# Fetching the first queries and keys in transfers of their own, on two queues, with other planning figures

## The chip, the cores and the metric

The program runs on one core of one Trainium2 chip. The metric is the device time of one execution in microseconds; less is better. In the profile PE is the tensor engine (PEld its weight loads), DVE VectorE, ACT ScalarE, POOL GpSimd, and SP the engine that issues transfers.

## What is computed

Attention with two sparse masks, then two networks on its output, all in float32:

```python
# q, k, v: (4, 8, 576, 64)
scores = scale * q @ k.T                      # per batch and head
mask_local   = (rel >= 0) & (rel < 32)        # heads 0 to 3, rel = query - key
mask_strided = (rel >= 0) & (key % 32 == query % 32)   # heads 4 to 7
attn = softmax(where(mask, scores, -1e9)) @ v
x = attn as (2304, 512)
h = maximum(maximum(x @ w1, x @ w2), x @ w3)  # 512 -> 768
x = h @ w_out                                 # 768 -> 512
h = x @ w_in                                  # 512 -> 2048
g = maximum(h, 0) + alpha * minimum(h, 0)
out = g @ w_out2                              # 2048 -> 512
```

## The kernel before

**Stages.** The program has three stages that share the engines in time. In the first, the attention of the four batches is woven with the first network ("gates": `w1`, `w2`, `w3` with their maximum; "mix": `w_out`) of batches 0 to 2 and with the conversion of the weights. Then the first network of batch 3 runs alone (`first_net`). In the last stage, from 403 us on, the second network runs in three blocks of 768 rows, whose products are written as seven per block and quarter (`h_products`) and followed by the output products (`o_units`). Products that have to be exact are done as three products of a high and a low part, so most matrices are split: a cast on ACT makes the high part, a subtraction on DVE the low one (L237 and L240 in the first stage).

**Attention.** It runs in units `(b, cc, hf)`: batch, a pair of heads, and half of the queries. Pairs 2 and 3 are the strided ones, 0 and 1 the local ones; the order of units in a batch is `ATT_UNITS` (2,0), (2,1), (3,0), (3,1), (0,0), (1,0), (0,1), (1,1). The strided queries and keys are stored by residue, so that a group of 6 or 7 residues is a block of 108 or 126 columns: three groups of 108 (324 columns) make the first half, two of 126 (252 columns) the second. A unit goes through scores on PE (L304), mask and row minimum on DVE (L312), exponential on ACT (L319), reciprocal on DVE (L330), scaling of `e` by `rc` on DVE or ACT (L252, L250), transposes on PE (L345), a copy `pt` to memory on either engine (L237), products with the values on PE (L370), and the split into `x` (L237, L240).

**Weights.** They arrive as 64-bit floats: a transfer `raw` (L413, three buffers), a word conversion on ACT (L427), a join on DVE (L431, L433), then the split into `w` (L237, L240). A gate group is twelve products of 288 columns (L530) with one weight tile; after it ACT or DVE takes the result into `t` (L616, L619). A group of the mix is 18 products (L552).

**What sets the order.** In the first stage a planner, `Weave`, sets it. Every piece of work is a task with an engine and a cost, a position `pos`, the events that it needs and gives, and the buffers that it makes and uses. `run` goes through time: among the tasks that are ready it takes, on the engine that is free first, the one with the smallest position, and emits its instructions there and then. `DELAY` is the time that the plan adds between the end of a task and its use elsewhere. Each engine then works through its own list in order. Buffers turn over in rings, eight banks of PSUM among them. All transfers are issued by SP, in the order of the plan, and wait there in line. The first is `alpha`, the slopes of the second network, which DVE negates into `nalpha` at the start of the last stage.

Of the kernel before, what the change touches and what calls it, by code (L numbers as in the profile page):

```python
# [2 lines left out]

# [19 lines left out]
NA = S // STRIDE  # L23
# [15 lines left out]
NUNITS = 2 * (3 * NF1 + NCC)  # L39
# [4 lines left out]
class Weave:  # L44
# [6 lines left out]

    DELAY = {"PE": 300, "ACT": 250, "DVE": 250, "SP": 2300}

    URGENT = 1000

    def __init__(self, rings):
# [33 lines left out]
                    at = max(at, done[u])  # L92
        return at

    def run(self):
        free = dict.fromkeys(self.DELAY, 0)
        left = [sum(len(self.givers[e]) for e in task[3]) for task in self.tasks]
        takers = {}
        for t, task in enumerate(self.tasks):
            for e in task[3]:  # L100
                for g in self.givers[e]:
                    takers.setdefault(g, []).append(t)
        at = [0] * len(self.tasks)
        ready = {t for t, n in enumerate(left) if not n}
        done, mode = {}, None
        while ready:
            options = {}
            for t in ready:
                engines, _, pos, _, makes, m, slack = self.tasks[t]
                when = self.place(makes, done)  # L110
                if when is None:
                    continue
                when = max(when, at[t] + slack)
                best = None
                for e, cost in engines:
                    start = max(when, free[e])
                    if best is None or start + cost < best[0] + best[2]:
                        best = (start, e, cost)
                start, e, cost = best
                if m is not None:  # L120
                    start += 100 * (m != mode)
                options.setdefault(e, []).append((start, pos - (m is not None and m == mode), t, cost))
            pick = None
            for e, c in options.items():
                first = min(o[0] for o in c)
                o = min((o for o in c if o[0] <= first + 120), key=lambda o: (o[1], o[0], o[2]))
                if pick is None or o[0] < pick[1][0]:
                    pick = (e, o)
            e, (start, _, t, cost) = pick
            _, emit, _, _, makes, m, _ = self.tasks[t]  # L130
            ready.remove(t)
            emit(e)
            for ring, key in makes:
                self.made[ring].append(key)
            mode = mode if m is None else m
            free[e] = start + cost
            done[t] = start + cost + self.DELAY[e]
            for u in takers.get(t, ()):
                left[u] -= 1
                same = e == "PE" == self.tasks[u][0][0][0]  # L140
                at[u] = max(at[u], start + cost if same else done[t])
                if not left[u]:
                    ready.add(u)
        assert len(done) == len(self.tasks)


@with_exitstack
def attention_maxout_prelu_kernel(
# [13 lines left out]
    nc = tc.nc  # L162
# [106 lines left out]
    def load_task(b, cc, pos):  # L269
        qk, vk = ("q", b, cc), ("v", b, cc)  # L270

        def emit_qk(_):
            q = qkp.tile([P, S], F32, tag="q", name="q")
            nc.sync.dma_start(q, qT[b, cc])
            k = qkp.tile([P, S + 32 * (cc < 2)], F32, tag="k", name="k")
            nc.sync.dma_start(k, kTl[b, cc] if cc < 2 else kTs[b, cc - 2])
            tl[qk] = q, k

        def emit_v(_):
            v = tl[vk] = vp.tile([P, 6 if cc < 2 else 5, 2, D], F32, tag="v", name="v")  # L280
            nc.sync.dma_start(v, vl[b, cc] if cc < 2 else vs[b, cc - 2])

        add(load(592), emit_qk, pos, gives=[qk], makes=[("q", qk)])
        add(load(350), emit_v, pos + 1, gives=[vk], makes=[("v", vk)])

    def attention_tasks(b, cc, hf, pos, step):
# [76 lines left out]
        def values(_):  # L363
# [6 lines left out]
                    nc.tensor.matmul(pv[D * j:D * (j + 1), nq * i:nq * (i + 1)], v[:nk, t, j, :],  # L370
                                     tl["pt", u, j][:nk, nq * i:nq * (i + 1)], start=True, stop=True)

        add((("PE", 2 * n * 85),), values, pos + 2 * step, needs=[vk] + [("pt", u, j) for j in range(2)],
            gives=[pvk], makes=[("bank", pvk)] + [("x", k) for k in fresh],
            uses=[vk] + [("pt", u, j) for j in range(2)] + xks, mode="values", slack=slack)

        def parts(h):
# [336 lines left out]

    homes = [("gate", f, g) for f in range(NF1) for g in range(3)] + [("mix", f) for f in range(NF1)]
    build_constants()
    nc.sync.dma_start(alpha_sb, alpha)
    for b in range(B):
        first, last = (-40, -8) if b == 0 else ((b - 1) * NUNITS + (16 if b == 1 else 3), b * NUNITS - 3)
        step = (last - first) / (len(ATT_UNITS) + 2)  # L720
        for i, (cc, hf) in enumerate(ATT_UNITS):
            if i in (0, 2, 4, 5):
                load_task(b, cc, first + step * i - 8)
            attention_tasks(b, cc, hf, first + step * i, step)
# [45 lines left out]
    ps_h = ctx.enter_context(tc.tile_pool(name="ps_h", bufs=2, space=PSUM, reuse_waits="tile"))  # L770
    ps_o = ctx.enter_context(tc.tile_pool(name="ps_o", bufs=6, space=PSUM, reuse_waits="tile"))
    NH = DM // 2
    nalpha = osp.tile([P, NF2], F32, name="nalpha")
    nc.vector.tensor_scalar(out=nalpha, in0=alpha_sb, scalar1=-1.0, scalar2=None, op0=ALU.mult)
    gts, kept, accs, res = {}, {}, {}, {}
# [300 lines left out]
```

## Time and profile before

| | |
|---|---|
| three timed runs | 770.6, 774.55, 776.38 us, median 774.55 |
| profiled execution | 772.29 us, its span 770.2 us |
| busy in the span | PE 97%, DVE 77%, ACT 59% |
| first matmul | 5.25 us |
| start of the last stage | 403.24 us |

Times inside the execution count from the start of the span. The profiled execution's own time is 2.1 us more than its span. Busy shares are means over stages with different limits; windows show the stages apart.

### The profile page before, as it was taken

The numbers are of one execution on the slowest core, as the hardware profiler recorded it, in microseconds if no ns is written. First come the engines' busy times: TensorE is split into PE (matmuls) and PEld (weight loads), VectorE is DVE, ScalarE is ACT, GpSimd is POOL, SyncE is SP. The second block draws the span as 40 slices with busy tenths as digits, with TensorE's granted clock in tenths as the row PEclk, the third lists the DMA queues.
The fourth block names the chain that finished last, engine by engine and source line by source line (L and its number), as shares of the span: only waits on it lengthen the run. The fifth ranks groups of instructions, "written<-read, shape, count | busy, mean of one in ns | idle before, by whom it ended". The sixth has DMA issues, their size and how long they took to land.

```text
span 770.2 us, 16100 instructions
## 1 busy us (share of the span) xinstructions
PE 744.1 (97%) x5704; PEld 723.2 (94%) x5704; DVE 594.6 (77%) x1658; ACT 457.9 (59%) x1238; POOL 3.2 (0%) x16
## 2 busy tenths in 40 slices
PE   5899999999989999999999999999999999999997
PEld 4689898999989999999999999999999999999997
DVE  5899998779777796326457988878888877888884
ACT  6997796656768487304246566634656644556561
POOL 1000000000000000000000000000000000000000
PEclk9899999999999999999999999999999999999999
DMA  7467768876879865365947789999888999877361
GB/s 243 157 233 250 222 233 289 297 247 247 291 262 310 274 205 170 120 243 209 342 157 249 264 290 304 381 393 364 286 286 311 347 403 327 271 250 255 119 204 53
DMA packets 85471, 199.37 MB, mean 259 GB/s; under 512 B 10640, under 2 KB 40848, under 8 KB 85392
## 3 DMA queue, kind: packets, MB, share of 16 engines
q1 hardware_dynamic: 85392, 198.35, 74.7%
q8 instruction: 45, 0.74, 0.4%
q14 instruction: 34, 0.28, 0.1%
HBM read 148.51 MB, written 49.81 MB: 258 GB/s over the span
## 4 chain that ended last, share of the span: by engine, by line
PE 60%; DVE 17%; DMA 10%; ACT 8%; issue 3%; SPq 1%; DVEq 0%; ACTq 0%
PE ph L947 20%; PE po L790 15%; PE bank L530 14%; PE bank L552 7%; DMA wh<-w 4%; ACT e L319 2%; DVE word L433 2%; DVE g L784 2%; DMA raw<-in_w 2%; DVE c L794 2%; DVE w L240 2%; PE bank L304 1%; DVE word L431 1%; DVE t L619 1%; PE bank L370 1%
## 5 line engine op out<-in xcount | busy, mean ns | idle before, releaser
L530 PE MATMUL bank<-x,w 128*128 128x288 f32 x1728 | 236.8, 297 | 4.5 <-DVE x L240 1.4
L530 PEld LDWEIGHTS bank<-x,w 128*128 128x128 f32 x1728 | 231.3, 189 | 6.7 <-ACT pt L237 1.7
L947 PE MATMUL ph<-x,w 128*128 128x384 f32 x1008 | 203.3, 337 | 1.1 <-DVE c L952 1.1
L790 PE MATMUL po<-w,g 128*128 128x256 f32 x1296 | 183.8, 282 | 1.7 <-DVE g L784 0.6
L790 PEld LDWEIGHTS po<-w,g 128*128 128x128 f32 x1296 | 175.5, 189 | 4.2 <-DVE g L784 3.2
L947 PEld LDWEIGHTS ph<-x,w 128*128 128x128 f32 x1008 | 168.3, 188 | 2.1 <-DVE c L952 1.8
L952 DVE TENSOR_TENSOR c<-ph,c 128x384 f32<-128x384 f32 x168 | 90.8, 553 | 33.1 <-PE ph L947 32.2
L783 ACT CAST g<-c 128x384 fp32r<-128x384 f32 x96 | 48.5, 505 | 89.7 <-DVE c L934 56.5
L552 PE MATMUL bank<-h,w 128*128 128x288 f32 x576 | 79.5, 297 | 0.4 <-DVE t L619 0.4
L552 PEld LDWEIGHTS bank<-h,w 128*128 128x128 f32 x576 | 76.8, 188 | 1.5 <-DVE t L619 0.6
L240 DVE TENSOR_TENSOR w<-word,w 128x512 fp32r<-128x512 f32 x88 | 55.4, 635 | 26.8 <-ACT w L237 26.5
L319 ACT ACTIVATE e<-e,nm 96x128 f32<-96x128 f32 (+2 forms) x176 | 67.9, 392 | 8.1 <-DVE nm L312 8.0
L904 ACT ACTIVATE c<-c 128x384 f32<-128x384 f32 x96 | 50.4, 525 | 34.0 <-DVE c L952 33.0
L237 ACT CAST w<-word 128x512 fp32r<-128x512 f32 x88 | 50.8, 582 | 31.8 <-DMA wh<-w 15.9
L905 ACT ACTIVATE c<-c,nalpha 128x384 f32<-128x384 f32 x96 | 59.2, 617 | 3.1
L908 DVE SCALAR_TENSOR_TENSOR c<-c 128x384 f32<-128x384 f32 x96 | 52.9, 551 | 8.9 <-ACT c L905 8.9
L784 DVE TENSOR_TENSOR g<-c,g 128x384 fp32r<-128x384 f32 x96 | 52.7, 549 | 1.9 <-ACT g L783 1.9
L784 DVE TENSOR_TENSOR g<-k,g 128x384 fp32r<-128x384 f32 x72 | 36.7, 548 | 14.4 <-ACT g L783 14.4
L427 ACT ACTIVATE word<-raw 128x512 f32<-128x512 f32 x56 | 37.2, 676 | 9.6 <-DMA raw<-in_w 4.8
L433 DVE SCALAR_TENSOR_TENSOR word<-raw,word 128x512 uint32<-128x512 uint32 x56 | 38.8, 692 | 1.9
L619 DVE TENSOR_TENSOR t<-bank,t 128x288 f32<-128x288 f32 x72 | 32.3, 449 | 7.6 <-PE bank L530 4.1
L783 ACT CAST g<-k 128x384 fp32r<-128x384 f32 x72 | 33.4, 516 | 7.8 <-PE po L790 4.4
(72 smaller groups left out, 683.3 us busy)
## 6 DMA issues: line engine op xcount, KB each, us to landing
w<-wh SPq DMA_DIRECT2D x72, 512.0 KB, 4.9
raw<-in_w SPq DMA_DIRECT2D x50, 512.0 KB, 4.6
w<-wo SPq DMA_DIRECT2D x48, 512.0 KB, 5.8
w<-wp SPq DMA_DIRECT2D x36, 512.0 KB, 6.0
wh<-w SPq DMA_DIRECT2D x24, 512.0 KB, 3.5
xd<-xst SPq DMA_DIRECT2D x28, 384.0 KB, 3.3
x<-xd SPq DMA_DIRECT2D x28, 384.0 KB, 8.1
wp<-w SPq DMA_DIRECT2D x24, 256.0 KB, 3.2
```

Of the source, the lines that this page charges most:

```text
L240: nc.vector.tensor_tensor(out=out_, in0=x, in1=y, op=ALU.subtract)
L319: nc.scalar.activation(tl[ek][:nq, j, i, :nk], tl[ek][:nq, j, i, :nk], AF.Exp, bias=tl["nm", u][:nq, j, i:i + 1], scale=-1.0, accum_out=tl ...
L433: nc.vector.scalar_tensor_tensor(out=a, in0=raw[:, :, 0], scalar=29, in1=a, op0=ALU.logical_shift_right, op1=ALU.bitwise_or)
L530: nc.tensor.matmul(acc, words["gate", f, g][:, wi, cc * P:(cc + 1) * P], xt[b, cc, hf][:, xi, :], start=n == 0, stop=n == 3 * NCC - 1)
L552: nc.tensor.matmul(acc, words["mix", f][:, wi, dc * P:(dc + 1) * P], st["h", hf, f][:, xi, :], start=n == 0, stop=n == 3 * NF1 - 1)
L783: nc.scalar.copy(g[:, 0], x)
L784: return g, lambda: nc.vector.tensor_tensor(out=g[:, 1], in0=x, in1=g[:, 0].bitcast(F32), op=ALU.subtract)
L790: nc.tensor.matmul(bank[:, NH * half:NH * (half + 1)], g[:, gi, t * P:(t + 1) * P], w[:, wi, off:off + NH], start=first and i == 0, stop=l ...
L905: nc.scalar.activation(a, a, AF.Copy, scale=nalpha[:, f:f + 1])
L908: nc.vector.scalar_tensor_tensor(out=a, in0=h, scalar=0.0, in1=a, op0=ALU.max, op1=ALU.add)
L947: nc.tensor.matmul(bank, words["h", n, i][:, wi, off + c * P:off + (c + 1) * P], x2h[blk, k, c][:, xi, :], start=m == 0, stop=m == 5)
L952: nc.vector.tensor_tensor(out=out_, in0=bank, in1=other, op=ALU.add)
```

## The change

Four things. The two transfers for the queries and keys of the first unit's pair, (0, 2), are cut at column 324: the first 324 columns of the queries are SP's first transfer and those of the keys ACT's first instruction; the other 252 columns follow on SP. `alpha` is fetched at the start of the last stage instead of the start of the program. The planner's hand-over time from ACT and DVE is 350 instead of 250, and the positions of batch 0's attention begin at -32 instead of -40. And the value products of a strided pair's second half now need those of its first half. `plan` also takes arguments for other settings; here they keep their defaults, and the random sway is zero.

```diff
-    DELAY = {"PE": 300, "ACT": 250, "DVE": 250, "SP": 2300}
...
+    def plan(self, seed=None, near=120, change=100, slack=1.0, delay=350, shift=0.0):
+
+        rng = random.Random(seed)
+        sway = [rng.uniform(-shift, shift) if task[2] > -self.URGENT / 2 else 0.0 for task in self.tasks]
+        delays = {"PE": 300, "ACT": delay, "DVE": delay, "SP": 2300}
...
-            nc.sync.dma_start(q, qT[b, cc])
             k = qkp.tile([P, S + 32 * (cc < 2)], F32, tag="k", name="k")
-            nc.sync.dma_start(k, kTl[b, cc] if cc < 2 else kTs[b, cc - 2])
+            source = kTl[b, cc] if cc < 2 else kTs[b, cc - 2]
+
+            cut = RG[3][0] * NA if (b, cc) == (0, 2) else 0
+            if cut:
+                nc.sync.dma_start(q[:, :cut], qT[b, cc][:, :cut])
+                nc.scalar.dma_start(k[:, :cut], source[:, :cut])
+            nc.sync.dma_start(q[:, cut:], qT[b, cc][:, cut:])
+            nc.sync.dma_start(k[:, cut:], source[:, cut:])
...
-        add((("PE", 2 * n * 85),), values, pos + 2 * step, needs=[vk] + [("pt", u, j) for j in range(2)],
-            gives=[pvk], makes=[("bank", pvk)] + [("x", k) for k in fresh],
+        begun = ("x begun", b, cc)
+        add((("PE", 2 * n * 85),), values, pos + 2 * step,
+            needs=[vk] + [("pt", u, j) for j in range(2)] + ([begun] if cc >= 2 and hf else []),
+            gives=[pvk] + ([begun] if cc >= 2 and not hf else []), makes=[("bank", pvk)] + [("x", k) for k in fresh],
...
-    nc.sync.dma_start(alpha_sb, alpha)
     for b in range(B):
-        first, last = (-40, -8) if b == 0 else ((b - 1) * NUNITS + (16 if b == 1 else 3), b * NUNITS - 3)
+        first, last = (-32, -8) if b == 0 else ((b - 1) * NUNITS + (16 if b == 1 else 3), b * NUNITS - 3)
...
     NH = DM // 2
+    nc.sync.dma_start(alpha_sb, alpha)
     nalpha = osp.tile([P, NF2], F32, name="nalpha")
```

What this does to the lists of the engines shows at three places. Line numbers after the change are higher: L320 are scores, L361 transposes, L386 value products, L548 gates, L570 the mix.

SP's list at the start of the program, before and then after; `in_qT` and `in_kTs` are the queries and the strided keys, `in_vs` the values.

```order
L717 DMA alpha_sb<-in_alpha 128x16
L274 DMA q<-in_qT 128x576
L276 DMA k<-in_kTs 128x576
L281 DMA v<-in_vs 128x640
L274 DMA q<-in_qT 128x576
L276 DMA k<-in_kTs 128x576
```

```order
L289 DMA q<-in_qT 128x324
L291 DMA q<-in_qT 128x252
L292 DMA k<-in_kTs 128x252
L297 DMA v<-in_vs 128x640
L291 DMA q<-in_qT 128x576
L292 DMA k<-in_kTs 128x576
```

The transfer of alpha is gone from the first place, the first queries are there in its stead, and the first 324 columns of keys are missing from the list, since ACT issues them; all that follows keeps its place.

PE's list at the end of batch 0's attention, before and then after: transposes (`ident,e`), value products (`pt,v`), scores (`k,q`) and the gates (`x,w`).

```order
L530 MATMUL bank<-x,w 128x288 x12
L370 MATMUL bank<-pt,v 64x96 x6
L304 MATMUL bank<-k,q 126x126 x4
L530 MATMUL bank<-x,w 128x288 x12
L345 MATMUL bank<-ident,e 128x96 x6
L304 MATMUL bank<-k,q 108x108 x6
L370 MATMUL bank<-pt,v 64x96 x6
L530 MATMUL bank<-x,w 128x288 x156
```

```order
L548 MATMUL bank<-x,w 128x288 x12
L386 MATMUL bank<-pt,v 64x96 x6
L361 MATMUL bank<-ident,e 128x96 x6
L320 MATMUL bank<-k,q 126x126 x4
L320 MATMUL bank<-k,q 108x108 x6
L386 MATMUL bank<-pt,v 64x96 x6
L548 MATMUL bank<-x,w 128x288 x228
```

One gate group less stands ahead of the last value products, and the run of gates behind them is 228 products long instead of 156.

PE's list at the end of batch 2's attention (the second boundary between batches), before and then after; `h,w` is the mix.

```order
L304 MATMUL bank<-k,q 108x108 x6
L370 MATMUL bank<-pt,v 64x96 x12
L345 MATMUL bank<-ident,e 128x96 x12
L530 MATMUL bank<-x,w 128x288 x12
L370 MATMUL bank<-pt,v 64x96 x12
L552 MATMUL bank<-h,w 128x288 x54
L530 MATMUL bank<-x,w 128x288 x24
```

```order
L320 MATMUL bank<-k,q 108x108 x6
L386 MATMUL bank<-pt,v 64x96 x12
L361 MATMUL bank<-ident,e 128x96 x12
L570 MATMUL bank<-h,w 128x288 x18
L386 MATMUL bank<-pt,v 64x96 x12
L570 MATMUL bank<-h,w 128x288 x54
L548 MATMUL bank<-x,w 128x288 x96
```

Between the transposes and the last value products there is now a group of the mix instead of a gate group. At the first boundary, a batch earlier, the new list has four score products between the transposes and the gate group, where there was nothing.

## Rows read from the trace of the kernel before

**Rows 1.** Windows: start:end, length, busy PE, PEld, DVE, ACT, POOL, PEclk, DMA, GB/s.

```profile
5.25:44.48 39.23, 31.73 (x278) 24.93 (x278) 31.84 (x196) 34.95 (x150) 0.00 (x0) 0.91 0.61 206
44.48:125.20 80.72, 78.36 (x654) 74.58 (x655) 76.47 (x231) 65.91 (x198) 0.00 (x0) 1.00 0.74 246
```

**Rows 2.** Waits of PE, 30 to 420 us: total, times, longest.

```profile
PE bank L345 <- DVE t L619: 1.4, 1, 1.4
PE bank L530 <- DVE x L240: 1.4, 1, 1.4
PE bank L530 <- ACT pt L237: 1.3, 2, 1.1
PE bank L345 <- ACT e L250: 1.0, 2, 0.6
```

**Rows 3.** Timeline, first 8 us: start, duration, engine, operation, idle time before it.

```profile
0.74 0.40 SPq L717 DMA_DIRECT2D alpha_sb<-in_alpha  x1
1.20 0.42 SPq L274 DMA_DIRECT2D q<-in_qT  x1
1.67 0.42 SPq L276 DMA_DIRECT2D k<-in_kTs  x1
...
3.08 0.43 SPq L276 DMA_DIRECT2D k<-in_kTs  x1
...
3.91 0.33 POOL L188 TENSOR_SCALAR_AFFINE_SELECT mask_s<-mask_s 128x126 f32<-128x126 f32 x1
...
5.25 2.30 PE L304 MATMUL bank<-k,q 64*108 64x108 f32 x20 [5.25 <-DMA k<-in_kTs]
...
7.11 0.38 ACT L319 ACTIVATE e<-e,nm 108x108 f32<-108x108 f32 x1 [5.09 <-DVE nm L312]
```

**Rows 4.** Issues up to 2 us, then to 3.5: size, us from issue to landing.

```profile
q<-in_qT SPq DMA_DIRECT2D x1, 288.0 KB, 3.1
k<-in_kTs SPq DMA_DIRECT2D x1, 288.0 KB, 3.5
alpha_sb<-in_alpha SPq DMA_DIRECT2D x1, 8.0 KB, 1.7
...
k<-in_kTs SPq DMA_DIRECT2D x1, 288.0 KB, 5.0
```

**Rows 5.** Groups by shape on ACT, 7.1 to 41.8 us: busy, mean ns, idle before.

```profile
L319 ACT ACTIVATE e<-e,nm 108x108 f32<-108x108 f32 x17 | 6.3, 373 | 5.1 <-DVE nm L312 5.1
...
L427 ACT ACTIVATE word<-raw 128x512 f32<-128x512 f32 x5 | 3.3, 670 | 0.0
...
L250 ACT ACTIVATE e<-e,rc 96x128 f32<-96x128 f32 x9 | 3.0, 397 | 0.0
...
L237 ACT COPY pt<-bank 128x288 f32<-128x288 f32 x4 | 1.5, 387 | 0.3 <-PE bank L345 0.2
...
L250 ACT ACTIVATE e<-e,rc 126x126 f32<-126x126 f32 x2 | 0.7, 400 | 0.0
```

**Rows 6.** Timeline of ACT and PE at the end of batch 0's attention.

```profile
41.45 0.38 ACT L237 COPY pt<-bank 128x288 f32<-128x288 f32 x1
...
44.48 20.68 PE L530 MATMUL bank<-x,w 128*128 128x288 f32 x154 [0.81 <-DVE w L240]
```

**Rows 7.** Timeline of PE: a score group, then the second and third boundary.

```profile
65.65 0.71 PE L304 MATMUL bank<-k,q 64*126 64x126 f32 x8
...
222.05 3.13 PE L530 MATMUL bank<-x,w 128*128 128x288 f32 x12 [1.08 <-ACT pt L237]
...
314.84 2.66 PE L552 MATMUL bank<-h,w 128*128 128x288 f32 x18
```

**Rows 8.** Timeline of SP, PE and DVE at the start of the last stage.

```profile
388.77 15.45 SPq L563 DMA_DIRECT2D x<-xo  x12
...
403.24 6.44 PE L947 MATMUL ph<-x,w 128*128 128x384 f32 x36
...
405.59 0.56 DVE L952 TENSOR_TENSOR c<-ph,c 128x384 f32<-128x384 f32 x1 [4.22 <-PE ph L947]
```

More of the change, by code (lines that the diff above doesn't have):

```diff
@@ L1 @@
 import math
+import random
 from contextlib import ExitStack
@@ L93, in place @@
         return at
-    def run(self):
-        free = dict.fromkeys(self.DELAY, 0)
-        left = [sum(len(self.givers[e]) for e in task[3]) for task in self.tasks]
[L98 to L102, printed above, removed]
+    def plan(self, seed=None, near=120, change=100, slack=1.0, delay=350, shift=0.0):
+        rng = random.Random(seed)
+        sway = [rng.uniform(-shift, shift) if task[2] > -self.URGENT / 2 else 0.0 for task in self.tasks]
+        delays = {"PE": 300, "ACT": delay, "DVE": delay, "SP": 2300}
+        self.made = {ring: [] for ring in self.rings}
+        free = dict.fromkeys(delays, 0)
+        left = [sum(len(self.givers[e]) for e in task[3]) for task in self.tasks]
         at = [0] * len(self.tasks)
         ready = {t for t, n in enumerate(left) if not n}
-        done, mode = {}, None
+        done, mode, order = {}, None, []
         while ready:
@@ L108, in run @@
             for t in ready:
-                engines, _, pos, _, makes, m, slack = self.tasks[t]
+                engines, _, pos, _, makes, m, wait = self.tasks[t]
                 when = self.place(makes, done)
@@ L112, in run @@
                     continue
-                when = max(when, at[t] + slack)
+                when = max(when, at[t] + slack * wait)
                 best = None
@@ L120, in run @@
                 if m is not None:
-                    start += 100 * (m != mode)
-                options.setdefault(e, []).append((start, pos - (m is not None and m == mode), t, cost))
+                    start += change * (m != mode)
+                options.setdefault(e, []).append(
+                    (start, pos + sway[t] - (m is not None and m == mode), t, cost))
             pick = None
@@ L125, in run @@
                 first = min(o[0] for o in c)
-                o = min((o for o in c if o[0] <= first + 120), key=lambda o: (o[1], o[0], o[2]))
+                o = min((o for o in c if o[0] <= first + near), key=lambda o: (o[1], o[0], o[2]))
                 if pick is None or o[0] < pick[1][0]:
@@ L129, in run @@
             e, (start, _, t, cost) = pick
-            _, emit, _, _, makes, m, _ = self.tasks[t]
+            makes, m = self.tasks[t][4:6]
             ready.remove(t)
-            emit(e)
+            order.append((t, e))
             for ring, key in makes:
@@ L136, in run @@
             free[e] = start + cost
-            done[t] = start + cost + self.DELAY[e]
-            for u in takers.get(t, ()):
+            done[t] = start + cost + delays[e]
+            for u in self.takers.get(t, ()):
                 left[u] -= 1
@@ L144, in run @@
         assert len(done) == len(self.tasks)
+        return order
+    def run(self, **settings):
+        self.takers = {}
+        for t, task in enumerate(self.tasks):
+            for e in task[3]:
+                for g in self.givers[e]:
+                    self.takers.setdefault(g, []).append(t)
+        for t, e in self.plan(**settings):
+            self.tasks[t][1](e)
 @with_exitstack
```

## The prediction

> **What bounds the kernel now.** I read the windows first [rows 1]. Between 44.48 and 125.20 the tensor engine (PE) is busy 78.36 of 80.72 us. The stage ahead of that is different: of the 39.23 us from the first matmul at 5.25 to 44.48 PE shows 31.73 us, at a mean granted clock of 0.91, while ScalarE (ACT) shows 34.95 and VectorE (DVE) 31.84. So the head of the program is a chain of scores, masks, exponentials and copies that ACT carries, and PE becomes the bound at 44.48. From there one run of 154 gate products takes 20.68 us, 134 ns each [rows 6]. The list of waits [rows 2] then says what PE loses from 30 to 420: single waits of up to 1.4 us. A gain can come from two places only, the head and those waits. The order of the last stage does not change, apart from one new wait, for alpha.
>
> The profiled execution took 772.29 us with a span of 770.2; the median of the three timed runs is 774.55, 2.3 us above it. I sum differences on the profiled execution and apply them to the median. The three runs spread from 770.6 to 776.38, so about 1% (7.7 us) is what a measurement can tell from no change.
>
> **Part 1, the first transfers.** Now SyncE (SP) issues alpha at 0.74, q at 1.20 and k at 1.67 [rows 3]; they land after 1.7, 3.1 and 3.5 us [rows 4], so k is there at 5.17 and PE starts at 5.25. After the change the first 324 of 576 columns of q are SP's first issue (0.74), and the same part of k is ACT's first instruction, at about the same moment, ahead of its table load. A 288 KB transfer lands after 3.1 us and an 8 KB one after 1.7, so 280 KB cost 1.4 us, 5 ns per KB. Both parts are 162 KB: 1.7 + 324 x 0.005 = 3.3 us, landing at 0.74 + 3.3 = 4.0. That is an estimate from these two rows. First matmul at 4.1 instead of 5.25: 1.15 us earlier. The ends: 2.0 us (each part for itself, 0.74 + 2.5 = 3.2) and 0 (no row shows a transfer from ACT's queue; it may be as late as k is now). I take the case that counts all bytes. The mask is finished at 3.91 + 0.33 = 4.24 [rows 3], and DVE starts on it well over a microsecond after PE, so it does not replace the wait. The second group of scores needs the other 252 columns, SP's second and third issues: by then the same 576 KB have been moved, by about 5.2, when PE is just through with the first group.
>
> Not all of this survives. The third group of scores needs the next q and k, whose places in SP's queue do not move (the k's is at 3.08); that k lands 5.0 us after its issue [rows 4], at 8.1. From a first score matmul to its first exponential it takes 7.11 - 5.25 = 1.86 us [rows 3], so ACT gets the third group at 8.1 + 1.86 = 9.95. Now it comes to it after ten exponentials of 0.373 us [rows 5], at 7.11 + 3.73 = 10.84. So 0.9 us of the earlier start are kept, however early the first transfers land.
>
> The rows also say that k lands 0.87 us after q (5.17 against 4.30), though it is issued only 0.47 later [rows 3 and 4]. The Trainium skill, "DMA: Bandwidth & Descriptors", section "Issuing engines are not separate DMA queues", says that the transfers of all issuing engines run on the same 16 DMA engines, and that a second issuing engine saves only the time of the issue. By that rule the use of ACT's queue alone would be worth one issue slot, 0.47 us, and the trace agrees as far as one queue can show it: the lag between q and k is data and not issue. By the rule alone the sum below would be some 0.4 us smaller.
>
> **Part 2, the new order in the head.** The planner now assumes 350 instead of 250 for a hand-over from ACT or DVE and places batch 0 later, so the order changes everywhere up to the last batch. In the head I compare what ACT does up to its last copy of batch 0's probabilities, which ends at 41.45 + 0.38 = 41.83 now [rows 6]. Counted in the two orders, the new one has 14 instead of 16 exponentials of 108x108, 4 instead of 5 word conversions, 6 instead of 4 copies of 128x288, and scalings of e by rc of 0 instead of 2 (126x126) and 6 instead of 9 (96x128); all other kinds are equal in number. With the means of [rows 5]: -2 x 0.373 - 0.67 + 2 x 0.387 - 2 x 0.400 - 3 x 0.397 = -2.6 us. Durations overlap a little with the next instruction's, so I take four fifths, 2.1 us (ends: 2.6, and 0 if ACT waits more than now). The last copy then ends at 41.83 - 0.9 - 2.1 = 38.8; the value products follow, some 0.7 us (an estimate, as long as the score group of [rows 7]), and the unbroken run of gates, 228 long in the new order, starts at 39.5. By then 12 gate products are done; the old order had 26 at 44.48. The 26th would be at 39.5 + 14 x 0.134 = 41.4, so the head gains 44.48 - 41.4 = 3.1 us, of which 0.9 is part 1. The five scalings have moved to DVE, which has two copies fewer for them and 7.4 us idle in that stretch [rows 1]; that hides them. Without that cover they are up to 2.0 us (0.40 each on ACT).
>
> What is late next is the supply of weights: each needs a join and a subtraction on DVE, and DVE shows 76.47 of 80.72 us in the stretch after 44.48 [rows 1]. The old run used its first three weights twice before it needed the fourth; so does the new one (five groups of twelve, 8.0 us). So the margin stays about what it is, if DVE's list is as far ahead as ACT's. That is the weakest step.
>
> **Part 3, the batch boundaries.** At the first one PE waits 1.4 us for x [rows 2]. The new order puts one more group of scores, 0.71 us [rows 7], between the transposes and the gate group that waits. I count -0.7 (ends 0 and -1.4). At the second one the last transposes and the next gate group wait 1.4 and 1.1 us [rows 2 and 7], and the gate group at 222.05 runs at half clock, 3.13 us [rows 7] against 12 x 0.134 = 1.6. Together 4.0 us. The new order has 18 output products there instead of the gate group, which is what the third boundary has already, and there they start without a wait (at 314.84) [rows 7]. But the wait for DVE's maximum, ahead of it, has no reason to go. I take half, -2.0 (ends 0 and -4.0).
>
> The new order will have waits of its own that I can't see in it. The nearest row is that of ACT's scalings, two waits of 1.0 in all [rows 2]. I take +1.2, between 0 and 4 (as much as could go).
>
> **Part 4, alpha moved.** Its transfer is now queued on SP behind the last store of the first net, which is issued by 388.77 + 15.45 = 404.22 [rows 8]. Landing 1.7 later [rows 4], at about 406.0, it lets nalpha run, and DVE's first sum of the last stage, at 405.59 now [rows 8], comes behind it, at 406.15. All that DVE has queued waits with it, above all that sum itself, which frees the second bank at about 406.7. PE's first three product groups, 6.44 / 6 = 1.07 us each from 403.24 [rows 8], end at 406.4, and the fourth needs that bank. Cost 0.3 us, or 1.2 with a landing of 2.6; I take 0.5, near the lower end, since little else is in flight there. The ordering edge for the second half of x costs nothing: the first half stands ahead of it in both orders.
>
> **Sum.** -3.1 - 0.7 - 2.0 + 1.2 + 0.5 = -4.1 us: 768.2 for the profiled execution, 770.4 for the median.
>
> **Rivals.**
> (a) *The weights become the bound.* DVE is 95% busy from 44.48 on, so PE, which starts its run earlier, catches up with DVE's list and waits. Then only the earlier start counts, less alpha and the new waits: -0.9 + 0.5 + 1.2, about 775.4. For it: DVE's share. Against: the run at 44.48 has 154 products without a wait.
> (b) *The first parts land no earlier*, because ACT's first transfer is slow or shares the engines with all that follows. Then 0.9 are missing: 771.3. Against it: the bytes ahead of the first matmul nearly halve.
> (c) *All of the boundary waits go*, and the half clock with them: -3.1 - 1.4 - 4.0 - 1.0 (scalings) + 0.5 = -9.0, about 765.5, faster by over 1%.
> (d) *Slower: alpha comes late.* nalpha stands ahead of DVE's whole list for the last stage. If alpha takes 5 us to land, as k did at 3.08 with others in flight [rows 4], it is there at 409.2, the fourth product group starts at 410 instead of 406.4, and PE, having idled 3.6 us, may go on at half clock as at 222.05, 1.5 us more: +5.1 in place of +0.5. With (a) that is 780. It decides, against the forecast, from a landing of about 5 us on.
>
> **Chances.** Forecast 0.52, (a) 0.20, (b) 0.08, (c) 0.14, (d) 0.06. The range is 764.5 to 776.5: (c) below and (a) above, with a microsecond more on either side for the runs' own spread. Faster by over 1% (below 766.8) takes (c) and a tail of the forecast, 0.20; slower by over 1% (above 782.3) only the far end of (d), 0.03.
>
> **What would show it.** First matmul at about 4.1, third group's exponentials at about 10; the 228-product run beginning at 39 to 40 with no wait over 0.5 us in it (if it waits for w or for DVE's words, (a) is right); the gate group behind the first boundary's transposes waiting under 0.7 us; no half-clock stretch at the second; DVE's first sum of the last stage some 0.5 us behind where it was against PE. Wrong would be a head as long as before, or new waits on PE of over 4 us between 45 and 400.

## The result, and the profile after

The changed kernel took 766.91 us (median of seven runs, 764.54 to 768.77) against 774.48 for the kernel before beside it (seven runs, 770.6 to 776.38): a ratio of 0.9908, 95% interval 0.9883 to 0.9933. That is 7.6 us less, where 4.1 less (770.4) was predicted; the time lies inside the range. The profiled execution after is the longest of its seven, 768.77 us with a span of 766.6 at a mean granted clock of 0.989; that of before, 772.29 at 0.993, lies below the median of its kernel. So the two traces differ by 3.6 us of span and the medians by 7.6.

The windows of the kernel after, cut where the stages end (the columns are those of [rows 1]): the head, the way to the 54 products of the mix behind the first batch boundary, from there to the same place at the second, and on to the last stage.

```profile
3.96:43.18 39.22, 31.82 (x264) 25.43 (x265) 30.47 (x187) 31.77 (x135) 0.29 (x1) 0.83 0.57 185
43.18:128.97 85.79, 84.85 (x715) 81.54 (x713) 81.67 (x271) 69.42 (x219) 0.00 (x0) 0.98 0.77 249
128.97:221.33 92.36, 92.36 (x797) 89.81 (x795) 76.88 (x256) 62.24 (x200) 0.00 (x0) 1.00 0.79 270
221.33:399.44 178.11, 176.44 (x1417) 172.42 (x1415) 111.12 (x325) 90.26 (x267) 0.00 (x0) 1.00 0.70 237
399.44:766.60 367.16, 360.52 (x2520) 356.82 (x2520) 298.35 (x632) 200.54 (x407) 0.00 (x0) 1.00 0.81 281
```

And the same stretches of the kernel before; its head is the first of [rows 1].

```profile
44.48:128.15 83.67, 81.31 (x691) 77.22 (x691) 79.32 (x246) 68.86 (x213) 0.00 (x0) 1.00 0.74 249
128.15:226.25 98.10, 94.58 (x798) 91.17 (x797) 78.85 (x272) 64.19 (x208) 0.00 (x0) 0.98 0.78 264
226.25:403.24 176.99, 176.02 (x1423) 173.13 (x1422) 106.47 (x315) 87.68 (x263) 0.00 (x0) 1.00 0.67 228
403.24:770.20 366.96, 360.40 (x2522) 356.71 (x2520) 298.11 (x631) 200.91 (x408) 0.00 (x0) 1.00 0.80 281
```

Take length minus busy PE in each. Before: 5.25 ahead of the first matmul, then 7.50, 2.36, 3.52 and 0.97 idle; after: 3.96, 7.40, 0.94, 0 and 1.67. Up to the last stage PE is idle 5.6 us less (19.60 against 13.97), but it is busy 1.8 us more (385.5 against 383.6) on the same products, since more of them run at a low clock. That is the 3.8 us by which the last stage starts earlier. The head, where the prediction saw its largest gain, has none: 39.22 us long in both, and at its end fewer gate products are done (12 instead of 26).

**Why the head gained nothing.** The first matmuls and transposes on PE after, with DVE's steps between them (start, duration, engine, operation, idle time before it):

```profile
3.96 1.42 PE L320 MATMUL bank<-k,q 64*108 64x108 f32 x12 [3.96 <-DMA k<-in_kTs]
5.83 1.22 PE L320 MATMUL bank<-k,q 64*126 64x126 f32 x8 [0.45 <-DMA k<-in_kTs]
8.60 1.42 PE L320 MATMUL bank<-k,q 64*108 64x108 f32 x12 [1.55 <-DMA k<-in_kTs]
10.02 0.27 DVE L328 CUSTOM_DVE_ANT_0 e<-bank,mask_s 108x108 f32<-108x108 f32 x1 [2.05 <-PE bank L320]
11.17 0.17 DVE L346 TENSOR_SCALAR rc<-sm 108x6 f32<-108x6 f32 x1
11.60 1.21 DVE L262 TENSOR_SCALAR e<-e,rc 108x108 f32<-108x108 f32 x6
12.02 1.30 PE L361 MATMUL bank<-ident,e 108*108 108x108 f32 x6 [2.00 <-DVE e L262]
```

PE starts at 3.96 instead of 5.25 [rows 3], as predicted. The third group of scores waits 1.55 us for the second pair's keys and starts at 8.60. DVE's list has that group's six masks ahead of the first unit's reciprocal and scalings (11.17, 11.60), so the first transposes come at 12.02. Before, these two were at 8.17 and 11.59:

```profile
8.17 1.42 PE L304 MATMUL bank<-k,q 64*108 64x108 f32 x12 [0.62 <-DMA k<-in_kTs]
11.59 1.30 PE L345 MATMUL bank<-ident,e 108*108 108x108 f32 x6 [2.00 <-DVE e L252]
```

The DMA views say why the third group is late: the cut parts land after 3.0 and 3.2 us, and the second pair's keys, issued at 3.08 as before, 5.4 us after it, where [rows 4] has 5.0.

```profile
k<-in_kTs ACTq DMA_DIRECT2D x1, 162.0 KB, 3.2
q<-in_qT SPq DMA_DIRECT2D x1, 162.0 KB, 3.0
...
k<-in_kTs SPq DMA_DIRECT2D x1, 288.0 KB, 5.4
```

The rest of the head is slow on PE itself. Two windows of the kernel after; the granted clock is the third number from the end:

```profile
22.90:26.30 3.40, 3.40 (x31) 2.55 (x31) 3.00 (x20) 3.32 (x14) 0.00 (x0) 0.54 0.02 5
29.70:39.90 10.20, 9.40 (x66) 7.94 (x64) 9.34 (x50) 9.27 (x37) 0.00 (x0) 0.51 0.39 130
```

Some 13.6 us lie at about the lower level, 1.2 GHz; the head before had one such stretch, from 27.2 to 34.0 at 0.52. ACT waits longer for PE there. Its waits from the first exponential's to the last copy of probabilities, first before, then after:

```profile
ACT e L319 <- DVE nm L312: 5.1, 1, 5.1
ACT x L237 <- PE bank L370: 1.7, 2, 1.0
ACT pt L237 <- PE bank L345: 0.2, 1, 0.2
```

```profile
ACT e L335 <- DVE nm L328: 4.0, 2, 3.4
ACT x L247 <- PE bank L386: 2.7, 4, 1.3
ACT pt L247 <- PE bank L361: 1.8, 3, 0.9
```

ACT's first exponential is 1.27 us earlier (5.84 against 7.11 [rows 3]). Behind it ACT waits 0.6 us for the third group (4.0 less the 3.4 ahead of that first exponential) and 1.0 and 1.6 us more than before for PE, 3.2 in all. Its last copy ends at 41.89, before at 41.83 [rows 6]: the stretch is 1.33 us longer with 3.2 more of waiting, so its work is 1.9 us less.

**The boundaries and the last stage.** PE's waits from 30 to 420 us, after, in answer to [rows 2]: the gates' waits for x and for pt are gone, and that of the transposes for t is down from 1.4 to 0.3. The longest, 1.1 us for another t ahead of the last 288 gate products (341.49), is not new: it is the last line below, from the kernel before, at 346.01 there.

```profile
PE bank L548 <- DVE t L559: 1.1, 1, 1.1
PE bank L361 <- ACT e L260: 0.8, 1, 0.8
...
PE bank L361 <- DVE t L637: 0.3, 1, 0.3
```

```profile
PE bank L530 <- DVE t L541: 1.0, 1, 1.0
```

The first boundary, the second, and the start of the last stage, after, in answer to [rows 7] and [rows 8]:

```profile
124.51 2.85 PE L548 MATMUL bank<-x,w 128*128 128x288 f32 x12
127.29 1.74 PE L386 MATMUL bank<-pt,v 128*64 128x96 f32 x24
...
217.60 2.66 PE L570 MATMUL bank<-h,w 128*128 128x288 f32 x18
220.19 1.21 PE L386 MATMUL bank<-pt,v 128*64 128x96 f32 x24
...
399.44 2.87 PE L965 MATMUL ph<-x,w 128*128 128x384 f32 x15 [0.53 <-ACT xo L657]
...
401.58 0.17 DVE L792 TENSOR_SCALAR nalpha<-alpha_sb 128x16 f32<-128x16 f32 x1 [5.34 <-DMA alpha_sb<-in_alpha]
401.90 0.56 DVE L970 TENSOR_TENSOR c<-ph,c 128x384 f32<-128x384 f32 x1
```

At the first one the gate group and the value products run at half clock, 2.85 and 1.74 us. PE waits nowhere at the second, and there the same value products take 1.21. DVE's first sum stands 2.46 us behind PE's start (2.35 before), so alpha costs nothing that can be seen.

### The profile page after: what moved, and what is told of

Read it like the earlier page. It is cut to its first block, busy times and chain, and to the rows that moved or that the text cites. A ratio compares the mean times of both kernels' runs of the same rounds, so it can differ in the third digit from the quotient of the medians.

```text
span 766.6 us, 16098 instructions
## 1 busy us (share of the span) xinstructions
PE 746.0 (97%) x5704; PEld 726.0 (95%) x5704; DVE 598.5 (78%) x1670; ACT 455.5 (59%) x1226; POOL 3.2 (0%) x16
## 4 chain that ended last, share of the span: by engine, by line
PE 78%; DVE 11%; DMA 5%; ACT 3%; issue 2%; SPq 1%; DVEq 0%; ACTq 0%
PE bank L548 27%; PE ph L965 20%; PE po L808 15%; PE bank L570 9%; PE bank L320 3%; PE bank L386 3%; PE bank L361 2%; DVE g L802 2%; DVE c L812 2%; DMA xs<-x 2%; DMA x<-xd 1%; DVE c L970 1%; DMA w<-wh 1%; ACT g L801 1%; ACT c L923 1%
## 5 line engine op out<-in xcount | busy, mean ns | idle before, releaser
L548 PE MATMUL bank<-x,w 128*128 128x288 f32 x1728 | 237.2, 297 | 1.1 <-DVE t L559 1.1
L548 PEld LDWEIGHTS bank<-x,w 128*128 128x128 f32 x1728 | 231.8, 190 | 3.0 <-DVE t L559 1.4
L570 PE MATMUL bank<-h,w 128*128 128x288 f32 x576 | 80.0, 297 | 0.0
L570 PEld LDWEIGHTS bank<-h,w 128*128 128x128 f32 x576 | 77.0, 188 | 1.1 <-issue 0.2
L451 DVE SCALAR_TENSOR_TENSOR word<-raw,word 128x512 uint32<-128x512 uint32 x56 | 38.8, 692 | 1.9
```

Of the source, the lines that this page charges most:

```text
L548: nc.tensor.matmul(acc, words["gate", f, g][:, wi, cc * P:(cc + 1) * P], xt[b, cc, hf][:, xi, :], start=n == 0, stop=n == 3 * NCC - 1)
L570: nc.tensor.matmul(acc, words["mix", f][:, wi, dc * P:(dc + 1) * P], st["h", hf, f][:, xi, :], start=n == 0, stop=n == 3 * NF1 - 1)
```

## The experiments

Each ran in several executions beside the kernel before; ratios are to that, with their intervals. The kernel before took 772.86 us (median) beside the runs with the transfers, the order, the hand-over and the heavy filling, 772.22 beside those with the position, the light filling, the earlier keys and the changed kernel again, 772.93 beside the next three, and 771.50 beside the last.

**The transfers without the order.** The kernel before with the cut transfers and the late alpha, its planning figures as they were:

```diff
+            cut = RG[3][0] * NA if (b, cc) == (0, 2) else 0
+            if cut:
+                nc.sync.dma_start(q[:, :cut], qT[b, cc][:, :cut])
+                nc.scalar.dma_start(k[:, :cut], source[:, :cut])
...
-    nc.sync.dma_start(alpha_sb, alpha)
...
+    nc.sync.dma_start(alpha_sb, alpha)
```

> The kernel before with the cut transfers and the moved alpha alone, in the old order of work. Theory A (the gain lies in the order after the head): first matmul near 4.0, second boundary as before with its waits and half clock, time 0.3 to 1.5 us below before, ratio 0.998 to 1.000. Rival B (the earlier start makes the gain, since each later list is shifted by it): 4 us or more below before, ratio 0.995 or less.

Measured: 774.02 us, ratio 1.0019 (0.9999 to 1.0039). The transfers gain nothing. The theory's second boundary isn't in the trace: the gate group there waits 0.84 us and runs at the full clock (1.86 us). At the first boundary it waits 2.30 us, and the value products behind it run at half clock, 2.19 us against 1.21 in the kernel before. PE in its trace:

```profile
3.97 2.30 PE L310 MATMUL bank<-k,q 64*108 64x108 f32 x20 [3.97 <-DMA k<-in_kTs]
7.94 1.42 PE L310 MATMUL bank<-k,q 64*108 64x108 f32 x12 [1.68 <-DMA k<-in_kTs]
11.36 1.29 PE L351 MATMUL bank<-ident,e 108*108 108x108 f32 x6 [2.00 <-DVE e L252]
...
45.16 1.07 PE L536 MATMUL bank<-x,w 128*128 128x288 f32 x6 [0.79 <-DVE w L240]
```

Of 1.28 us at the first matmul 0.23 are left at the first transposes; at the run of gates, which waits for weights here as it does before [rows 6], there is nothing left.

**The order without the transfers.** The changed kernel with the old first transfers and alpha first:

```diff
+            nc.sync.dma_start(q, qT[b, cc])
...
-            cut = RG[3][0] * NA if (b, cc) == (0, 2) else 0
...
+            nc.sync.dma_start(k, kTl[b, cc] if cc < 2 else kTs[b, cc - 2])
...
+    nc.sync.dma_start(alpha_sb, alpha)
...
-    nc.sync.dma_start(alpha_sb, alpha)
```

> The changed kernel with the old first transfers: whole q and k on SP and alpha first, so only the planning figures and the ordering edge are new. Theory A: first matmul at 5.25, no wait and no half clock at the second boundary, 6 to 7 us below before, ratio 0.991 to 0.993. Rival B: at most 3 us below before, ratio 0.996 or more.

Measured: 764.04 us, ratio 0.9901 (0.9874 to 0.9928), as good as the whole change. The gain is the order's.

**Each planning figure by itself.** First the hand-over alone:

```diff
-    DELAY = {"PE": 300, "ACT": 250, "DVE": 250, "SP": 2300}
+    DELAY = {"PE": 300, "ACT": 350, "DVE": 350, "SP": 2300}
```

> The kernel before with the hand-over time of 350 alone; positions, transfers and alpha as before. Its list has the mix group at the second boundary, as the changed kernel has, but at the first boundary the old list without the scores in between. Theory A (the second boundary's waits and half clock are worth 4 us): second boundary without a wait, 3 to 5 us below before, ratio 0.994 to 0.996. Rival C (the gain is from batch 0's positions or from waits elsewhere): within 1 us of before.

Measured: 767.02 us, ratio 0.9932 (0.9910 to 0.9955). Theory A's reason isn't in the trace: at the second boundary PE still waits (0.69 and 0.48 us), and the mix group runs at half clock, 4.18 us against 2.66 in the changed kernel. Then the position alone:

```diff
-        first, last = (-40, -8) if b == 0 else ...
+        first, last = (-32, -8) if b == 0 else ...
```

> The kernel before with batch 0's positions from -32 alone; hand-over time 250, transfers and alpha as before. Its list has a score group and a mix group at the first boundary, but scores and a gate group at the second. If the two planning figures simply add up (theory A: the new figures are worth what the waits at the boundaries are worth), it is 1.5 to 3 us below before, ratio 0.996 to 0.998, with no long wait at the first boundary and one of 1 to 2 us with half clock at the second. Rival G (the figures only work together): within 1 us of before.

Measured: 765.78 us, ratio 0.9921 (0.9897 to 0.9945). Theory A is out too: the gain is over twice what it allowed, and the trace has no wait at the second boundary, where it had put 1 to 2 us. Each figure brings most of the gain, and they don't add: 0.68 and 0.79%, together 0.9 to 1.0.

**The clock of the head, with too much filling.** The changed kernel with six products of the identity with itself ahead of each half unit's transposes of batch 0 (their result is overwritten):

```diff
+                if b == 0:
+                    for _ in range(6):
+                        nc.tensor.matmul(tr[:, :P], ident, ident, start=True, stop=True)
```

> The changed kernel with six extra 128x128 products ahead of each pair of transposes of batch 0, into the bank that the transposes then overwrite; the output is the same. Theory D (the half clock in the head costs what the new list of ACT should have saved there): granted clock near 1.0 from 20 to 40 us, the 228-product run begins at 40 to 41 instead of 43.2, time 1 to 3 us below the changed kernel's median of 766.9. Rival E (the head waits on hand-overs between engines, whatever the clock): the run begins at 43 or later, and the extra products cost 0 to 4 us.

Measured: 776.09 us, ratio 1.0055 (1.0029 to 1.0082). That is slower than either theory allowed. The clock column shows the upper level throughout the head, but the products stand in the way; the window of its head (to the run of 228):

```profile
3.90:52.63 48.73, 45.70 (x457) 41.88 (x457) 30.03 (x187) 31.91 (x135) 0.33 (x1) 1.00 0.50 163
```

**Light filling.** Four such products at four places where PE waits anyway, and the changed kernel itself once more beside it:

```diff
+                if (u, j) in (((0, 2, 0), 0), ((0, 3, 0), 1), ((0, 0, 0), 1), ((0, 0, 1), 0)):
+                    for _ in range(4):
+                        nc.tensor.matmul(tr[:, :P], ident, ident, start=True, stop=True)
```

> The changed kernel with four extra 128x128 products (about 1 us) ahead of four transposes of batch 0 at which PE sat idle for 0.8 to 2.0 us, into the bank that the transposes overwrite; the output is the same. Theory D (the half clock in the head is what spreads the runs between 764.5 and 768.8 and what costs the head): granted clock near 1.0 between 15 and 45 us, the 228-product run at 41 or earlier, all runs near 764. Rival E: the clock is up, but the run begins at 43 as before and the time is 767 or more.

> The changed kernel again, beside these. If the clock in the head decides (theory D), its runs are again spread with the mean granted clock: about 764.5 at 0.998, about 768.5 at 0.989, and the run of 228 products begins earlier where the head has less half clock. Otherwise the spread has no relation to the clock.

Measured: 762.35 us with the filling (761.69 to 764.03), ratio 0.9870 (0.9844 to 0.9897), and 764.88 for the changed kernel (763.5 to 767.45), ratio 0.9903 (0.9876 to 0.9931). The head's window with the filling, and then that of the changed kernel beside it, each to its run of 228:

```profile
3.96:37.60 33.64, 29.35 (x297) 23.66 (x297) 28.86 (x181) 30.70 (x135) 0.28 (x1) 1.00 0.63 212
```

```profile
4.06:41.55 37.49, 28.56 (x264) 22.46 (x264) 29.24 (x181) 30.78 (x132) 0.18 (x1) 0.95 0.56 190
```

With the filling PE has 33 more records, the clock column stays at the upper level, 2.4 GHz, and the run of 228 starts 3.95 us earlier; the first profiled execution of the changed kernel, with 0.83 in its head, had it at 43.18. Part of the 3.95 is the third group's start (8.16 with the filling, 9.28 beside it). Two other traces separate the two: the run of the order alone and the last experiment below are the same program but for the filling, their third groups start at 8.28 and 8.25, and the head's windows, each to its run of 228, differ by 2.85 us:

```profile
5.18:41.03 35.85, 28.55 (x264) 22.93 (x264) 29.67 (x187) 31.71 (x135) 0.00 (x0) 0.90 0.58 194
5.16:38.16 33.00, 30.08 (x296) 24.46 (x296) 28.86 (x181) 30.36 (x133) 0.00 (x0) 1.00 0.63 208
```

The medians of the filled kernel and of the one beside it differ by 2.5 us; the ranges overlap by 0.5. The spread with the mean clock did not come again: of the six runs beside it the one at 0.998 took 766.61 us and the one at 0.991 764.43.

**The second pair's keys earlier.** The changed kernel with the first pair's values issued behind the second pair's queries and keys:

```diff
+            if (b, cc) == (0, 3):
+                nc.sync.dma_start(tl["v", 0, 2], vs[0, 0])
...
+            if (b, cc) != (0, 2):
+                nc.sync.dma_start(v, vl[b, cc] if cc < 2 else vs[b, cc - 2])
```

> The changed kernel with the first pair's values issued behind the second pair's queries and keys on SP. Theory H (the earlier start is lost because DVE's list has the masks of the third score group ahead of the first unit's scalings, and that group waits for keys issued sixth): the third group starts at 7.2 to 7.6 instead of 8.6, the first transposes at 10.7 to 11.1 instead of 12.0, the 228-product run correspondingly 1 us earlier than in a run of the changed kernel with the same clock, time 0.5 to 1.5 us below the changed kernel. Rival (ACT or the clock decides in the head): the first transposes earlier, the run not, and no difference in time.

Measured: 763.30 us (761.47 to 764.47), ratio 0.9884 (0.9855 to 0.9913), 1.6 under the changed kernel beside it. Both traces have a mean clock of 0.95 in the head, so they can be set against each other. With the keys earlier, and then the changed kernel beside it:

```profile
7.11 1.42 PE L323 MATMUL bank<-k,q 64*108 64x108 f32 x12 [0.76 <-DMA k<-in_kTs]
10.52 1.30 PE L364 MATMUL bank<-ident,e 108*108 108x108 f32 x6 [2.00 <-DVE e L262]
```

```profile
9.28 1.42 PE L320 MATMUL bank<-k,q 64*108 64x108 f32 x12 [2.49 <-DMA k<-in_kTs]
12.69 1.30 PE L361 MATMUL bank<-ident,e 108*108 108x108 f32 x6 [2.00 <-DVE e L262]
```

The third group comes 2.17 us earlier and the first unit's transposes, which need none of its keys, come earlier by the same 2.17: they hang on that group through DVE's list. Not all of the 2.17 is the edit's, since 9.28 is late; other traces with the cut transfers and the old place of the keys had 7.94 to 9.21. The run of 228 starts at 38.45 instead of 41.55. The medians differ by half of that; the intervals of their ratios overlap.

**Both together.** The two edits above in one kernel:

> The changed kernel with both repairs of its head: the first pair's values issued behind the second pair's queries and keys, and four extra identity products ahead of four of the transposes of batch 0. Apart they took 1.6 and 2.5 us off the changed kernel beside them (764.88). Theory 1, the two losses are separate: they add, about 760.8 us, with the run of 228 gate products at about 35. Theory 2, both bring the run of 228 to about 38 and from there the supply of weights bounds it: about 762.3, as with the extra products alone, and PE waits for w inside the run.

Measured: 762.65 us, ratio 0.9868 (0.9840 to 0.9896). The median shows no sum, though its interval just reaches 760.8. The trace says more: the run of 228 starts at 36.98, where the earlier keys alone had 38.45 and the filling alone 37.60; the first theory wanted 35. But it waits for no weights either, which was the second theory's reason. Both edits shorten the same stretch. In this trace the gate group at the first boundary runs at half clock (3.04 us, 1.85 with the filling alone), which takes back what the run of 228 is ahead; the three profiled spans are 759.5, 759.7 and 759.9. What bounds the kernel then was not tried.

**The filling in the old order.** The kernel before with the same four fillings:

> The kernel before with four extra identity products ahead of the same four transposes of batch 0, its order and transfers unchanged. Theory 1, the half clock in the head costs the old order as much as the new one: the granted clock of the head is 1.0 and the time is about 2.5 us under that of the kernel before. Theory 2, the old order's head is carried by ACT and not by PE: no gain, within 1 us of the kernel before, though the clock is full; its run of 154 gate products begins at 44 to 45 as it does now. If the extra products stand in PE's way they add up to 16 x 0.25 = 4 us.

Measured: 768.14 us (765.98 to 772.4), ratio 0.9944 (0.9922 to 0.9966). That is 4.8 us under the kernel before, more than either theory had. The old order's head was slowed by the clock too: its run of 154 starts at 42.10 instead of 44.48, and waits 0.81 us for weights as before. Three windows of its trace, its head, the way to the first boundary's mix and that to the second's:

```profile
5.29:42.10 36.81, 32.34 (x311) 25.98 (x311) 31.53 (x196) 34.28 (x150) 0.00 (x0) 1.00 0.66 221
42.10:128.38 86.28, 83.48 (x690) 78.83 (x690) 79.97 (x246) 68.48 (x211) 0.00 (x0) 0.98 0.74 241
128.38:221.52 93.14, 92.48 (x798) 89.52 (x797) 77.81 (x269) 63.49 (x205) 0.00 (x0) 1.00 0.80 278
```

The last is telling. It is the list of the kernel before, which took 98.10 us there in the trace of before; here, with nothing changed in that stretch, it takes 93.14. In the run with the transfers alone it took 93.64:

```profile
133.01:226.65 93.64, 92.80 (x798) 89.85 (x797) 76.65 (x267) 62.35 (x201) 0.00 (x0) 1.00 0.79 276
```

The gate group at that boundary waits 0.66 us here and runs at the full clock:

```profile
218.59 1.85 PE L533 MATMUL bank<-x,w 128*128 128x288 f32 x12 [0.66 <-ACT pt L237]
```

**Without the ordering edge.** The changed kernel without the need for the first half's value products:

```diff
-            needs=[vk] + [("pt", u, j) for j in range(2)] + ([begun] if cc >= 2 and hf else []),
...
+            needs=[vk] + [("pt", u, j) for j in range(2)],
...
```

> The changed kernel without its last part, the need of a strided pair's second value products for those of the first half. The planner's order then differs from the first batch boundary on, by some ten places on PE. Theory 1, the part is worth nothing by itself: within 1 us of the changed kernel (764.9 beside the earlier runs). Theory 2, part of the gain at the second boundary comes from it: 767 or more, with waits there again.

Measured: 764.87 us, ratio 0.9902 (0.9873 to 0.9930). Nothing that these runs can tell hangs on it.

**Order and filling, with the old transfers.** The run of the order alone with the four fillings:

> The changed kernel with the old first transfers, alpha first on SP's queue (as in the run of the order alone) and four extra identity products ahead of four of the transposes of batch 0. With the extra products PE has its full clock through the head, so an earlier first matmul could come through. Theory 1, the cut transfers are worth nothing there either, since the third group's keys set the pace: within 1.5 us of the changed kernel with the same extra products, a ratio to the kernel before of 0.986 to 0.989. Theory 2, they are worth their 1.1 us and more once the head is dense: 1.5 us or more above it, a ratio of 0.989 or more.

Measured: 763.36 us, ratio 0.9883 (0.9846 to 0.9921). The run of 228 starts at 38.16, against 37.60 with the cut transfers. Of the 1.2 us at the first matmul 0.1 is left at the first transposes (11.58 against 11.49); the rest of the 0.56 comes later, where the next score group takes 1.22 us here and 0.71 there. The medians can tell nothing of it.

This trace and that of the old order with the filling have the same transfers and the same clock column in the head, so they show what the order does there. The window to the first boundary's mix:

```profile
38.16:124.24 86.08, 85.03 (x715) 81.47 (x713) 82.38 (x278) 69.60 (x221) 0.00 (x0) 0.98 0.76 249
```

Counted from the first matmul to the 26th gate product (14 of the run's, 1.9 us), the head takes 34.9 us in the new order and 36.81 in the old. Up to 0.6 of the 1.9 can be the old execution's later third group (8.97, 3.7 us behind its first matmul, against 8.25, 3.1 behind). From there to the first mix the new order takes 84.2 and the old 86.28, to the second 92.32 and 93.14, to the last stage 176.68 and 176.42. So of 4.7 us by which the last stage starts earlier, about 4 lie ahead of the first boundary's mix. It is one execution of each.

## Why the prediction was right in its time and wrong in its places

**The total.** The forecast of a gain within 1% held, with 4.1 us where 7.6 were measured. The reason given for most of it, the head, is not what the profile of the changed kernel shows: its head is as long as before, which the prediction itself had named as a sign of being wrong. That the time lies in the range is in part luck. Of the rivals, (c) is nearest, with 765.5 against 766.91, but not by its terms: 3.1 us of it are that head, and 4.0 the second boundary of one execution.

**"0.9 us of the earlier start are kept" failed.** The first matmul came at 3.96 (4.1 predicted). I had seen that the third group's keys don't move, but followed them into ACT's exponentials, where there was slack. The path runs through DVE: its list puts the third group's masks ahead of the first unit's reciprocal and scalings, so everything waits for those keys. Where the keys came 2.17 us earlier, so did the first transposes; that is shown. The transfers' missing 0.9 was rival (b)'s result, but by another cause than (b)'s: the parts did land earlier. The Trainium skill, "DMA: Bandwidth & Descriptors", section "Issuing engines are not separate DMA queues", had a second queue save an issue slot only. The trace agrees as far as landings go (162 KB in 3.2 us on ACT's queue and 3.0 on SP's); the first matmul gained 1.29 us, more than one issue slot; with the queue the bytes and alpha's place changed too, and no run parts them.

**The 2.1 us of ACT's work** were there as work (about 1.9 less) and not as time: ACT waited 2.6 us more for PE. I had named that end ("0 if ACT waits more than now") and not asked what would make it wait. It was in large part the clock: with the filling the last copy ends at 36.42 and the run of 228 starts at 37.60, both earlier than predicted (38.8 and 39.5), and of two traces with the same third group the one at 1.00 has a head 2.85 us shorter than the one at 0.90. Set against the old order with the filling, the new head gains 1.9 us, or 1.3 without the later third group there. So the term's mechanism is right where PE keeps up, and it was no part of what the profiled execution gained. How much of it the other executions have is not shown: in the first seven runs the two with a mean clock of 0.998 took 764.54 and 764.83 us and the two with 0.989 768.35 and 768.77, but the repeat does not follow that.

**The second boundary, -2.0.** The pair of traces shows more, 5.7 us of that stretch (98.10 to 92.36). But the old list took 93.64 and 93.14 there in two other kernels. The new list's 92.36 is 0.8 and 1.3 better than those. So most of what I priced belonged to one execution and not to the old order. The failing step is the one that took the waits of one profile for a property of the list. The 1.5 us for the half clock were also too high: a gate group at a boundary takes 1.88 us at the full clock (at 125.20), not 1.6, so 3.13 is 1.25 more.

**The first boundary, -0.7.** PE's idle time up to its mix fell from 2.36 to 0.94, but the gate group and the value products there took 2.85 and 1.74 us at half clock, 1.0 and 0.5 more than at the full one (1.85 and 1.21 in the repeat). The waits did what was said, and in that execution the clock took it back.

**New waits, +1.2, and alpha, +0.5.** Idle time between the second boundary and the last stage rose by 0.7; the last stage took 367.16 instead of 366.96. By this pair the terms were too high by 0.5 and 0.3; the stretch from the second boundary to the last stage, waits and work together, is 1.1 us longer. Rival (d) is out: alpha was in use 1.8 us after its issue.

**Rival (a), the weights,** is refuted: the run of 228 has no wait inside, at 43.18 and when it starts at 36.98.

**Where the gain is.** In the order, by the runs with and without it: 0.9901 with the order alone, 1.0019 with the transfers alone, and 0.9883 against 0.9944 with the clock of the head held up in both, so 0.6% has nothing to do with that clock. The two first traces put it in PE's idle time ahead of the last stage, and those with the filling put most of it ahead of the first boundary's mix; which waits make it up differs between executions of one list, as the second boundary shows. Why either planning figure alone brings most of it is not settled.

## What to carry to other kernels

Before costing an earlier transfer, walk the in-order list of every engine between it and the first result that is wanted: one instruction of a later group, waiting for a later transfer, gives back the whole start. Price a wait from more than one execution; one that another execution of the same list does not have is not the list's. And where PE idles in short pieces at the start, try a few idle-time products: here four at four places were worth about 2.5 us in the changed kernel and 4.8 in the one before, and six at every place cost some 11.

## What was not expected of the hardware

The clock in the head is granted differently from execution to execution of one program: 0.83 over 39.22 us in one, 0.95 over 37.49 in another. The Trainium skill, "TensorE: Matmul & The Clock Gate", Part 1, says of the slow matmuls at a kernel's start that their number varies between runs of the same kernel, and that this start costs under 1% of a typical span. The stretches here at 22.9 and 29.7 us come after the start and vary too; light filling gains 0.3% in the changed kernel and 0.6% in the one before, under 1%, but a third and more of what the whole change is worth.

In the first microseconds matmuls take longer than the clock column accounts for: the same twelve score records last 1.42 us at 8.60, where the page shows 1.00, and 0.82 at 119.33. Likewise the first four extra products took 2.08 us and the next four 1.07. The 1.42 us are what such a group takes at 32.54, where the column is at 0.51. How long this lasts differs: the group below still takes 1.60 us in the kernel after, where the column shows 1.00, but 0.90 at 14.59 with the filling and at 15.55 in the run without the ordering edge. So the mean clock of a head does not count all of its slow matmuls. No row here tells why.

```profile
16.71 1.60 PE L320 MATMUL bank<-k,q 64*96 64x128 f32 x12
```
